# Attention's softmax: dividing the values in place of the weights, and decoding later weights after attention

## The chip, the cores and the metric

The program runs on one core of a Trainium2 chip. A core has TensorE (PE in the rows, with PEld for its weight loads), VectorE (DVE), ScalarE (ACT), GpSimd (POOL) and SyncE (SP), which issues the transfers here. TensorE writes its results to PSUM, which the program uses as eight banks of 128 x 512 float32. The metric is the device time of one execution in microseconds (us); the lower, the better.

## The reference, cut to what matters

Three layers follow one another on 1152 rows of 512 numbers (2 batches x 576 positions, 8 heads x 64):

```python
# attention: a coarse one on means over 4 positions, repeated 4 times, plus a local one (|i - j| < 4)
def sm_attn(qq, kk, vv):
    s = scale * qq @ kk.T
    s = s - max(s)
    a = exp(s)
    a = a / (sum(a) + 1e-09)
    return a @ vv
attn_out = repeat(sm_attn(q_d, k_d, v_d), 4) + sm_attn_masked(q, k, v)
# first layer: h = x @ w_in, g = h * tanh(softplus(h)), x = g @ w_out    (512 -> 2048 -> 512)
# second: 8 experts of 512 -> 1024 -> 512, all on every row, weighted by a gate that is normalised 8 times
out = sum(P[:, e:e + 1] * (relu(x @ w1[e]) @ w2[e]) for e in range(8))
```

`w_in` and `w_out` arrive as float64, so the kernel reads them as pairs of 32-bit words and puts float32 numbers together from them.

## The kernel before, in words

**Three stages.** Attention is worked off in units: eight of the coarse kind (`gunit`: a batch, a half of its rows, four heads) and twelve of the local kind (`lunit`: 96 rows, all heads). Two coarse and three local units run by themselves at the start, with `warm` matmuls of the identity between them. The other units are woven into the first layer in three waves of two coarse and three local units each (the second batch's two halves, and the first batch's second half). The first layer runs over 64 chunks (`s` in the last loop of the quoted code; 12 matmuls of `gemm1`, line 506, then the activation `mish`, then 12 matmuls of `gemm2`, line 529, which belong to the chunk `LAG` = 4 before). The waves cover chunks 0 to 17, and `ATT_END` is 18. Afterwards the first layer runs alone, and then the experts (lines 783 and 821).

**A unit has three steps**: `sc` (scores, lines 321 or 363 and 368, then `softmax`), `tr` (transposes of the weights, line 335 or 379, copied from PSUM by ScalarE, line 337 or 380) and `av` (weights times values, line 347 or 386, then line 349 or lines 392 to 394, which write the first layer's input as a sum of two parts, `xhi` and `xlo`). `piped` puts the steps of different units between each other. `softmax` takes the maximum on VectorE (line 300), the exponentials and their sums on ScalarE (302), adds and inverts the sums (304, 305), and multiplies the weights by the reciprocals on VectorE (307, two instructions a unit).

**Decoding.** A half piece of `w_in` or `w_out` is loaded into one of two buffers (`load_w64`), and `w_raw` makes float32 of it by one ScalarE instruction (180) and three on VectorE (181, 183, 184). When it is done it asks for the load of the half piece four on, which waits until its buffer is free. `w_split` makes two parts of a whole piece (190 on ScalarE, 191 on GpSimd). There are 16 pieces, 32 half pieces; `need` says from which chunk a piece is used, and before the change a half piece is decoded from `AHEAD` = 22 chunks ahead. By the loop that gives the half pieces 12 to 19 to the chunks 7 to 14, under attention; they are used from chunk 24 on.

**What sets the order.** The code is written in program order, but a scheduler reorders the instructions within each engine's queue when the program is built, so the order on the chip is the one in the listings below. Each engine then works its queue off in that order. PSUM banks come in two rings of four, `w` and `acc`. Scores, transposes, values and `gemm1` share the ring `w`, and a bank is free for its next user only when its last reader is done: for `gemm1` that is line 490 of `mish`.

Of the kernel before, what the change touches and what calls it, by code (L numbers as in the profile page):

```python
# [7 lines left out]
F32 = mybir.dt.float32  # L8
# [3 lines left out]
AF = mybir.ActivationFunctionType  # L12
ALU = mybir.AluOpType
# [3 lines left out]
TQ = 96  # L17
# [4 lines left out]
NBUF = 3  # L22
RAWB = 4
ERAW = 3
AHEAD = 22
VWB = 3
PBL, PBG = 6, 4
WARM0, WARM1, WARM2 = 16, 8, 2
# [10 lines left out]
def attn_moe_moe_kernel(  # L39
# [13 lines left out]
    PE, ACT, DVE, POOL, SP = nc.tensor, nc.scalar, nc.vector, nc.gpsimd, nc.sync  # L53
    B, H, S, D = q.shape
# [3 lines left out]
    KD = DM // 128  # L58
# [3 lines left out]
    SD = S // 4  # L62
# [7 lines left out]
    W = TQ + 6  # L70
# [14 lines left out]
    def new(pool, shape, dt, tag, bufs=2):  # L85
        return pool.tile(shape, dt, tag=tag, name=tag, bufs=bufs)
# [15 lines left out]
    POOL.affine_select(out=maskb, in_=maskb, pattern=[[-1, W + 6]], base=9, channel_multiplier=1,  # L102
                       compare_op=ALU.is_ge, fill=NEG)
    vwt = [at.tile([W, H, D], F32, name=f"vw{i}", bufs=1) for i in range(VWB)]
    pl = [at.tile([TQ, H // 2, W], F32, name=f"pl{i}", bufs=1) for i in range(PBL)]
    pg = [at.tile([SH, H // 4, SD], F32, name=f"pg{i}", bufs=1) for i in range(PBG)]
    DVE.memset(two, 2.0)
    DVE.memset(ones, 1.0)
# [10 lines left out]
    def at_bank():  # L119
        state["n"] += 1  # L120
        return bank("acc" if state["start"] and state["n"] % 2 else "w")
# [172 lines left out]
    def softmax(s3, p, rows, tag):  # L294

        n, nh, nk = s3[0].shape
        den = new(at, [n, 2, nh], F32, tag + "d", 2)
        for par in range(2):
            nm = new(at, [n, nh], F32, tag + "m", 4)
            DVE.tensor_reduce(out=nm, in_=s3[par], axis=AX.X, op=ALU.max, negate=True)  # L300
            for i in range(nh):
                exps.append(ACT.activation(out=p[par][:, i], in_=s3[par][:, i], func=AF.Exp, bias=nm[:, i:i + 1],  # L302
                                           scale=1.0, accum_out=den[:, par, i:i + 1]))
        DVE.tensor_scalar(out=den, in0=den, scalar1=1e-9, scalar2=rows, op0=ALU.add, op1=ALU.mult)
        DVE.reciprocal(out=den, in_=den)
        for par in range(2):
            DVE.tensor_tensor(
                out=p[par], in0=p[par], in1=den[:, par].unsqueeze(2).to_broadcast([n, nh, nk]), op=ALU.mult)

    def gunit(b, half, q4):  # L310


        u = {}
        hps = (2 * q4, 2 * q4 + 1)

        def sc():
            bks = [at_bank() for _ in range(2)]
            for i, hp in enumerate(hps):
                for par, bk in enumerate(bks):
                    o = slice(64 * par, 64 * par + 64)  # L320
                    PE.matmul(out=bk[:SH, SD * i:SD * i + SD], lhsT=qd[b, half][o, hp, :], rhs=kd[b][o, hp, :],
                              start=True, stop=True)
            for par in range(2):
                u[par] = pg[state["pg"] % PBG]
                state["pg"] += 1
            softmax([bk[:SH, 0:2 * SD].rearrange("p (a b) -> p a b", b=SD) for bk in bks], u, 4.0, "g")

        def tr():
            u["pt"] = new(at, [W, 8 * TQ], F32, "pt", 2)[:SH, 0:8 * SH].rearrange("p (a b) -> p a b", a=8)
            for par in range(2):  # L330
                bk = at_bank()
                for i in range(2):
                    for c in range(2):
                        j = 2 * i + c
                        PE.transpose(out=bk[:SH, SH * j:SH * j + SH], in_=u[par][:, i, SH * c:SH * c + SH],
                                     identity=ident[:SH, :SH])
                ACT.activation(out=u["pt"][:, 4 * par:4 * par + 4, :].rearrange("p a b -> p (a b)"),
                               in_=bk[:SH, 0:4 * SH], func=AF.Copy)

        def av():  # L340
            if (b, half) not in odT:
                odT[b, half] = new(at, [128, HP, SH], F32, "odT", 1)
            bk = at_bank()
            for i, hp in enumerate(hps):
                for c in range(2):
                    for par in range(2):
                        PE.matmul(out=bk[64 * par:64 * par + 64, SH * i:SH * i + SH], lhsT=vd[b, c][:, 2 * hp + par, :],
                                  rhs=u["pt"][:, 4 * par + 2 * i + c, :], start=(c == 0), stop=(c == 1))
            ACT.activation(out=odT[b, half][:, hps[0]:hps[0] + 2, :].rearrange("p a b -> p (a b)"),
                           in_=bk[:, 0:2 * SH], func=AF.Copy)  # L350
        return [sc, tr, av]

    def lunit(t):

        b, t6, lo, hi = window(t)
        half, t3 = divmod(t6, 3)
        m0 = lo - (TQ * t6 - 6)
        u = {}

        def sc():  # L360
            s3 = [at_bank()[:TQ, 0:4 * W].rearrange("p (a b) -> p a b", b=W) for _ in range(2)]
            for par in range(2):
                PE.matmul(out=s3[par], lhsT=identb[:TQ, :TQ],  # L363
                          rhs=maskb[:TQ, m0:m0 + W].unsqueeze(1).to_broadcast([TQ, 4, W]), start=True, stop=False)
            for hp in range(HP):
                for par in range(2):
                    o = slice(64 * par, 64 * par + 64)
                    PE.matmul(out=s3[par][:, hp, :], lhsT=qT[b, half][o, hp, TQ * t3:TQ * t3 + TQ],  # L368
                              rhs=kT[b][o, hp, lo:hi], start=False, stop=(hp == HP - 1))
            for par in range(2):  # L370
                u[par] = pl[(2 * t + par) % PBL]
            softmax(s3, u, 1.0, "l")

        def tr():
            u["pt"] = new(at, [W, 8 * TQ], F32, "pt", 2)
            for par in range(2):
                bk = at_bank()
                for i in range(HP):
                    PE.transpose(out=bk[:W, TQ * i:TQ * i + TQ], in_=u[par][:, i, :], identity=ident[:TQ, :TQ])  # L379
                ACT.activation(out=u["pt"][:, 4 * TQ * par:4 * TQ * par + 4 * TQ], in_=bk[:W, 0:4 * TQ], func=AF.Copy)  # L380

        def av():
            bk = at_bank()
            for hp in range(HP):
                for par in range(2):
                    PE.matmul(out=bk[64 * par:64 * par + 64, TQ * hp:TQ * hp + TQ], lhsT=vw[t][:, 2 * hp + par, :],
                              rhs=u["pt"][:, TQ * (4 * par + hp):TQ * (4 * par + hp) + TQ], start=True, stop=True)
            y = bk[:, 0:KD * TQ].rearrange("p (a s) -> p a s", a=KD)
            y4 = bk[:, 0:KD * TQ].rearrange("p (a s r) -> p a s r", a=KD, r=4)
            g = odT[b, half][:, :, 24 * t3:24 * t3 + 24]  # L390
            hi_, lo_ = (z[:, :, TQ * t:TQ * t + TQ] for z in (xhi, xlo))
            DVE.tensor_tensor(out=y4, in0=y4, in1=g.unsqueeze(3).to_broadcast([128, KD, 24, 4]), op=ALU.add)
            ACT.activation(out=hi_, in_=y, func=AF.Copy)  # L393
            DVE.tensor_tensor(out=lo_, in0=y, in1=f32(hi_), op=ALU.subtract)
        return [sc, tr, av]
# [197 lines left out]
    for s in range(NS + LAG):  # L593
        if s == NS - 4:
            with tc.issue_after(last["mish"].ins):
                gate()
        for a, b, st in waves:
            if s == b:
                while steps:
                    steps.pop(0)()  # L600
            if s == b == waves[-1][1]:
                at_ctx.close()
                tp = ctx.enter_context(tc.tile_pool(name="tp", bufs=1, side="right", reuse_waits="tile"))
                tx["hi"], tx["lo"] = (tp.tile([128, 3 * KH, NB], F32R, name=f"t{z}") for z in ("hi", "lo"))
            if s == a:
                steps += st
                pump.n, pump.done, pump.at, pump.over = len(steps), 0, 24 * a, FRAC * 24 * (b - a)
        n = place["raw"] // 2
        if n < len(ring) and s >= need[ring[n]] - AHEAD and (s < ATT_END or s % 2 == 0 or s >= need[ring[n]] - 4):
            if s:  # L610
                with tc.issue_after(last["mish"].ins):
                    w_raw()
            else:
                w_raw()
                w_raw()
        n = place["split"]
        if n < len(ring) and 2 * n + 2 <= place["raw"] and free_at(n) <= s:
            w_split()
        if s < NS:
            gemm1(s)  # L620
        if s >= LAG:
            gemm2(s - LAG)
# [269 lines left out]
```

## Time and profile before

| | us |
|---|---|
| median of 3 runs | 1111.71 |
| lowest and highest | 1108.79, 1116.67 |
| the profiled execution | 1111.02 |
| its span, first to last instruction | 1109.2 |
| before the first `gemm1` matmul | 47.9 |
| chunks 0 to 17, with the three waves | some 48 to 187 |

The profiled execution took 1.8 us more than its span and stands 0.7 us under the median. PE is busy in 1077.7 us of the span, DVE in 579.6, ACT in 487.8 and POOL in 368.9, so TensorE bounds the whole. The change touches the first 190 us and, by the decoding, the 60 us behind them. A share of busy time says little there: which engine is waited for has to be read from the waits of that stretch.

### The profile page before, as it was taken

The numbers are of one execution on the slowest core, as the hardware profiler recorded it, in microseconds if no ns is written. First come the engines' busy times: TensorE is split into PE (matmuls) and PEld (weight loads), VectorE is DVE, ScalarE is ACT, GpSimd is POOL, SyncE is SP. The second block draws the span as 40 slices with busy tenths as digits, with TensorE's granted clock in tenths as the row PEclk, the third lists the DMA queues.
The fourth block names the chain that finished last, engine by engine and source line by source line (L and its number), as shares of the span: only waits on it lengthen the run. The fifth ranks groups of instructions, "written<-read, shape, count | busy, mean of one in ns | idle before, by whom it ended". The sixth has DMA issues, their size and how long they took to land.

```text
span 1109.2 us, 18583 instructions
## 1 busy us (share of the span) xinstructions
PE 1077.7 (97%) x7184; PEld 983.7 (89%) x7184; DVE 579.6 (52%) x1229; ACT 487.8 (44%) x1375; POOL 368.9 (33%) x406
## 2 busy tenths in 40 slices
PE   8889999999998999999999999999999999999998
PEld 7768789999998888988989898999888999889897
DVE  4877885545347554454454544435454444444442
ACT  3776777534446443424344242442424434243430
POOL 2444523402217335705134150431505224051300
PEclk9888999999999999999999999999999999999999
DMA  8374320222002102112011111201112011120002
GB/s 189 107 154 120 102 81 20 77 80 74 20 1 76 58 1 77 39 38 76 13 66 39 38 40 38 76 19 58 39 38 76 20 58 38 39 71 20 25 1 86
DMA packets 60196, 63.48 MB, mean 57 GB/s; under 512 B 24204, under 2 KB 44620, under 8 KB 60108
## 3 DMA queue, kind: packets, MB, share of 16 engines
q1 hardware_dynamic: 60108, 62.30, 18.8%
q8 instruction: 56, 0.92, 0.3%
q14 instruction: 32, 0.26, 0.1%
HBM read 59.93 MB, written 2.36 MB: 56 GB/s over the span
## 4 chain that ended last, share of the span: by engine, by line
PE 87%; DVE 4%; ACT 3%; POOL 2%; DMA 2%; issue 1%; POOLq 0%; DVEq 0%
PE w L821 36%; PE acc L783 26%; PE w L506 9%; PE acc L529 8%; PE w L783 4%; PE w L368 1%; ACT pl L302 1%; DMA raw<-in_k_dram 1%; PE acc L442 1%; DMA raw<-in_moe_w_out_dram 0%; POOL wc L695 0%; PE w L363 0%; PE w L379 0%; ACT raw L180 0%; POOL me L487 0%
## 5 line engine op out<-in xcount | busy, mean ns | idle before, releaser
L821 PE MATMUL w<-wc,hhi 128*128 128x512 f32 x1152 | 361.9, 393 | 0.0
L821 PEld LDWEIGHTS w<-wc,hhi 128*128 128x128 f32 x1152 | 210.4, 188 | 37.8
L821 PE MATMUL w<-wc,hlo 128*128 128x512 f32 x576 | 225.2, 391 | 0.0
L695 POOL TENSOR_TENSOR wc<-raw,wc 128x512 fp32r<-128x512 f32 x64 | 82.0, 1305 | 356.1 <-ACT wc L694 355.9
L783 PE MATMUL acc<-thi,wb 128*128 128x288 f32 x768 | 169.0, 295 | 0.0
L783 PE MATMUL acc<-xhi,wb 128*128 128x288 f32 x768 | 167.2, 295 | 1.7 <-DVE xlo L557 1.7
L832 DVE SCALAR_TENSOR_TENSOR yacc<-w,P,yacc 128x512 f32<-128x512 f32 x126 | 94.3, 749 | 81.1 <-PE w L821 81.1
L783 PEld LDWEIGHTS acc<-thi,wb 128*128 128x128 f32 x768 | 128.4, 188 | 3.1
L783 PEld LDWEIGHTS acc<-xhi,wb 128*128 128x128 f32 x768 | 128.1, 188 | 3.1 <-DVE xlo L557 1.9
L821 PEld LDWEIGHTS w<-wc,hlo 128*128 128x128 f32 x576 | 108.1, 188 | 23.8
L770 ACT ACTIVATE p<-acc 128x288 f32<-128x288 f32 x128 | 52.3, 410 | 143.2 <-PE acc L783 139.3
L774 ACT ACTIVATE hhi<-acc 128x288 fp32r<-128x288 f32 x128 | 52.3, 410 | 141.5 <-PE acc L783 117.3
L783 PE MATMUL acc<-xlo,wb 128*128 128x288 f32 x384 | 113.5, 295 | 0.0
L783 PE MATMUL acc<-tlo,wb 128*128 128x288 f32 x384 | 113.1, 295 | 0.0
L683 POOL TENSOR_TENSOR wb<-sums,wb 128x256 fp32r<-128x256 f32 x128 | 93.6, 748 | 53.5 <-ACT wb L682 52.1
L683 POOL TENSOR_TENSOR wb<-raw,wb 128x256 fp32r<-128x256 f32 x96 | 72.5, 758 | 97.4 <-PE acc L783 55.5
L775 DVE SCALAR_TENSOR_TENSOR hlo<-acc,hhi 128x288 fp32r<-128x288 f32 x128 | 58.2, 455 | 77.4 <-ACT hhi L774 74.9
L506 PE MATMUL w<-xhi,hi 128*128 128x288 f32 x256 | 79.4, 311 | 5.3 <-ACT xhi L393 2.9
L506 PE MATMUL w<-xlo,hi 128*128 128x288 f32 x256 | 77.7, 304 | 0.1
L529 PE MATMUL acc<-glo,hi 128*128 128x288 f32 x256 | 76.1, 303 | 1.4 <-POOL glo L494 1.4
L506 PE MATMUL w<-xhi,lo 128*128 128x288 f32 x256 | 77.3, 302 | 0.0
L796 DVE TENSOR_TENSOR acc<-acc,u 128x288 f32<-128x288 f32 x64 | 29.6, 464 | 87.7 <-PE acc L783 87.7
(192 smaller groups left out, 1992.9 us busy)
## 6 DMA issues: line engine op xcount, KB each, us to landing
raw<-in_moe_w_dram SPq DMA_DIRECT2D x64, 512.0 KB
raw<-in_moe_w_in_dram SPq DMA_DIRECT2D x16, 512.0 KB
raw<-in_moe_w_out_dram SPq DMA_DIRECT2D x16, 512.0 KB
vw<-in_v_dram SPq DMA_DIRECT2D x12, 192.0 KB
raw<-in_v_dram SPq DMA_DIRECT2D x8, 288.0 KB
raw<-in_q_dram SPq DMA_DIRECT2D x12, 144.0 KB
out_dram<-yacc SPq DMA_DIRECT2D x6, 256.0 KB
raw<-in_k_dram SPq DMA_DIRECT2D x2, 576.0 KB
```

Of the source, the lines that this page charges most:

```text
L302: exps.append(ACT.activation(out=p[par][:, i], in_=s3[par][:, i], func=AF.Exp, bias=nm[:, i:i + 1], scale=1.0, accum_out=den[:, par, i:i + ...
L506: PE.matmul(out=bk, lhsT=a[:, kk, o], rhs=b[:, kk, c0:c0 + n], start=(i == 0), stop=(i == 3 * KD - 1))
L529: PE.matmul(out=bk, lhsT=a[:, h, o], rhs=b, start=(first and i == 0), stop=(end and i == 2))
L683: POOL.tensor_tensor(out=t[:, 1], in0=src[u][w], in1=f32(t[:, 0]), op=ALU.subtract)
L695: POOL.tensor_tensor(out=t[:, 1], in0=r[:, a], in1=f32(t[:, 0]), op=ALU.subtract)
L770: ACT.activation(out=t, in_=bk[u, b], func=AF.Copy)
L774: ACT.activation(out=hi, in_=y, func=AF.Relu)
L775: DVE.scalar_tensor_tensor(out=lo, in0=y, scalar=0.0, in1=f32(hi), op0=ALU.max, op1=ALU.subtract)
L783: PE.matmul(out=bk[u, b], lhsT=wb[2 * h + u, w][:, wz, kk, :], rhs=ops[xz][:, k + kk, o + c:o + c + NP], start=(m < 3 and i == 0), stop=(i ...
L796: DVE.tensor_tensor(out=bk[u, "C"], in0=bk[u, "C"], in1=kept[u, "u2"], op=ALU.add)
L821: PE.matmul(out=bk, lhsT=a[:, f, 128 * j:128 * j + 128], rhs=w[:, b, :], start=(i == 0), stop=(i == 3 * FH - 1))
L832: DVE.scalar_tensor_tensor(out=y, in0=bk, scalar=p, in1=y, op0=ALU.mult, op1=ALU.add)
```

## The change

The weights stay as the exponentials give them. `softmax` returns the reciprocals (96 or 72 partitions, one column for each head), and `spread` lays each column out: a matmul whose stationary operand is the column repeated 64 times and whose moving operand is the identity puts the reciprocals of one head on 64 partitions, one column for each row of attention. `av` of a coarse unit spreads into its own bank and multiplies by it (ScalarE's copy, then one VectorE multiply). A local unit spreads in `tr` into a bank of its own, which ScalarE copies to `u["r"]` (over the unit's first weight tile), and multiplies its values in `av`. The pieces from the seventh on (half pieces 12 to 31) are decoded from chunk 18 on, one half piece in each chunk.

```diff
@@ softmax
-        den = new(at, [n, 2, nh], F32, tag + "d", 2)
+        den = new(at, [n, 2, nh], F32, tag + "d", 4)
...
         DVE.reciprocal(out=den, in_=den)
+        return den
+
+    def spread(bk, c, den, i):
+
+        n = den.shape[0]
         for par in range(2):
-            DVE.tensor_tensor(
-                out=p[par], in0=p[par], in1=den[:, par].unsqueeze(2).to_broadcast([n, nh, nk]), op=ALU.mult)
+            PE.matmul(out=bk[64 * par:64 * par + 64, c:c + n], lhsT=den[:, par, i:i + 1].to_broadcast([n, D]),
+                      rhs=ident[:n, :n], start=True, stop=True)
@@ gunit, av
-            ACT.activation(out=odT[b, half][:, hps[0]:hps[0] + 2, :].rearrange("p a b -> p (a b)"),
-                           in_=bk[:, 0:2 * SH], func=AF.Copy)
+                spread(bk, 2 * SH + SH * i, u["den"], i)
+            z = odT[b, half][:, hps[0]:hps[0] + 2, :].rearrange("p a b -> p (a b)")
+            ACT.activation(out=z, in_=bk[:, 0:2 * SH], func=AF.Copy)
+            DVE.tensor_tensor(out=z, in0=bk[:, 2 * SH:4 * SH], in1=z, op=ALU.mult)
@@ lunit, tr
+            bk = at_bank()
+            for hp in range(HP):
+                spread(bk, TQ * hp, u["den"], hp)
+            u["r"] = pl[2 * t % PBL].rearrange("p a b -> p (a b)")[:, 0:KD * TQ]
+            ACT.activation(out=u["r"], in_=bk[:, 0:KD * TQ], func=AF.Copy)
@@ lunit, av
+            DVE.tensor_tensor(out=bk[:, 0:KD * TQ], in0=bk[:, 0:KD * TQ], in1=u["r"], op=ALU.mult)
             DVE.tensor_tensor(out=y4, in0=y4, in1=g.unsqueeze(3).to_broadcast([128, KD, 24, 4]), op=ALU.add)
@@ the loop over chunks
-        if n < len(ring) and s >= need[ring[n]] - AHEAD and (s < ATT_END or s % 2 == 0 or s >= need[ring[n]] - 4):
+        if n < len(ring) and s >= (ATT_END if n >= 2 * NBUF else 0):
```

The built programs show where the instructions went. In the changed kernel the lines are numbered anew: 299 stands for 300, 303 and 304 for 304 and 305, 180 to 183 for 181 to 184, 500 to 504 for 488 to 492, 311 is `spread`, 353 is 347, 385 is 379, 518 is 506, and 541 is 529.

The first place is VectorE's queue around the first local unit of the first wave (`lm` are maxima, `ld` sums and reciprocals, `pl` weights, `raw` a piece that is decoded, `mm` and `me` belong to `mish`). Before:

```order
L305 RECIPROCAL ld<-ld 96x8
L300 TENSOR_REDUCE lm<-w 96x4
L307 TENSOR_TENSOR pl_94<-pl_94,ld 96x408
L307 TENSOR_TENSOR pl_95<-pl_95,ld 96x408
L300 TENSOR_REDUCE lm<-w 96x4
L181 TENSOR_SCALAR raw<-raw 128x512
L488 SCALAR_TENSOR_TENSOR mm<-me 128x288
L183 SCALAR_TENSOR_TENSOR raw<-raw_827,raw 128x512
L490 TENSOR_TENSOR me<-mm,w 128x288
```

And now:

```order
L304 RECIPROCAL ld<-ld 96x8
L299 TENSOR_REDUCE lm<-w 96x4
L180 TENSOR_SCALAR raw<-raw 128x512
L299 TENSOR_REDUCE lm<-w 96x4
L182 SCALAR_TENSOR_TENSOR raw<-raw_860,raw 128x512
L183 SCALAR_TENSOR_TENSOR raw<-raw_860,raw 128x512
L500 SCALAR_TENSOR_TENSOR mm<-me 128x288
L502 TENSOR_TENSOR me<-mm,w 128x288
```

The two multiplies are gone, and the decoding's last instruction has moved ahead of `mish`.

The second place is VectorE's queue at the coarse units of the second wave (`gm`, `gd` and `pg` are their maxima, sums and weights). Before:

```order
L181 TENSOR_SCALAR raw<-raw 128x512
L490 TENSOR_TENSOR me<-mm,w 128x288
L304 TENSOR_SCALAR gd<-gd 72x4
L183 SCALAR_TENSOR_TENSOR raw<-raw_1166,raw 128x512
L305 RECIPROCAL gd<-gd 72x4
L184 SCALAR_TENSOR_TENSOR raw<-raw_1166,raw 128x512
L307 TENSOR_TENSOR pg_100<-pg_100,gd 72x288
L307 TENSOR_TENSOR pg_101<-pg_101,gd 72x288
```

And now:

```order
L502 TENSOR_TENSOR me<-mm,w 128x288
L303 TENSOR_SCALAR gd<-gd 72x4
L299 TENSOR_REDUCE gm<-w 72x2
L304 RECIPROCAL gd<-gd 72x4
L504 TENSOR_TENSOR me<-me,ml 128x288
```

Both the decoding and the multiplies are gone from there.

The third place is TensorE's queue at the first `gemm2` (`acc<-ghi`, `acc<-glo`), among the scores of the first wave's coarse units (`w<-kd,qd`). Before:

```order
L321 MATMUL w<-kd,qd 72x144 x2
L529 MATMUL acc<-ghi,hi_835 128x288 x4
L321 MATMUL w<-kd,qd 72x144 x4
L529 MATMUL acc<-glo,hi_835 128x288
L529 MATMUL acc<-ghi,lo_836 128x288
```

And now:

```order
L325 MATMUL w<-kd,qd 72x144 x8
L541 MATMUL acc<-ghi,hi_868 128x288 x4
L518 MATMUL w<-xhi,hi_849 128x288
L518 MATMUL w<-xlo,hi_849 128x288
L518 MATMUL w<-xhi,lo_850 128x288
...
L541 MATMUL acc<-glo,hi_868 128x288
```

Ahead of the first `glo` now stands a whole chunk of `gemm1` (12 matmuls on `xhi` and `xlo`, of which the first three are shown), which stood some ten matmuls behind it before.

## Rows read from the trace of the kernel before

**Rows 1.** The page, part 4: shares of the chain that ended last, by engine

```profile
PE 87%; DVE 4%; ACT 3%; POOL 2%; DMA 2%; issue 1%; POOLq 0%; DVEq 0%
```

**Rows 2.** Four stretches: length, busy us of each engine (x instructions), clock, DMA

```profile
48.00:98.00 50.00, 44.25 (x331) 38.79 (x332) 38.32 (x78) 33.48 (x118) 19.52 (x18) 0.79 0.52 118
98.00:147.00 49.00, 42.69 (x397) 37.24 (x396) 42.19 (x88) 36.54 (x131) 25.11 (x27) 1.00 0.47 129
147.00:190.00 43.00, 42.00 (x377) 38.23 (x376) 30.46 (x69) 32.31 (x118) 12.30 (x13) 0.96 0.13 41
190.00:306.00 116.00, 116.00 (x877) 116.00 (x876) 53.58 (x97) 52.24 (x125) 30.80 (x26) 1.00 0.18 60
```

**Rows 3.** Waits of PE, 48 to 190 us: total, times, longest

```profile
PE w L506 <- ACT xhi L393: 2.9, 2, 1.7
PE acc L529 <- ACT ghi L493: 1.9, 1, 1.9
...
PE acc L529 <- POOL glo L494: 1.4, 2, 0.9
```

**Rows 4.** Stretches of 5 us, the same columns as in rows 2

```profile
60.00:65.00 5.00, 5.00 (x20) 4.35 (x20) 4.00 (x9) 3.32 (x13) 2.08 (x2) 0.50 0.87 166
...
80.00:85.00 5.00, 5.00 (x22) 3.79 (x22) 3.36 (x5) 2.43 (x8) 2.42 (x3) 0.50 0.31 108
85.00:90.00 5.00, 5.00 (x37) 4.66 (x37) 3.76 (x9) 2.95 (x16) 1.19 (x2) 0.56 0.18 58
...
100.00:105.00 5.00, 3.88 (x37) 3.60 (x37) 4.47 (x11) 3.68 (x11) 1.73 (x2) 1.00 0.65 181
105.00:110.00 5.00, 3.84 (x35) 3.46 (x34) 3.58 (x6) 3.12 (x9) 4.11 (x5) 1.00 0.74 200
...
115.00:120.00 5.00, 3.57 (x26) 2.65 (x22) 4.19 (x11) 4.61 (x20) 4.83 (x5) 1.00 0.46 132
120.00:125.00 5.00, 4.13 (x33) 3.27 (x34) 4.96 (x11) 2.56 (x6) 4.34 (x5) 1.00 0.34 105
```

**Rows 5.** PE in order of time: start, us, instruction, [idle before <-releaser]

```profile
76.78 0.87 PE L379 MATMUL w<-ident,pl 96*102 96x96 f32 x8 [0.75 <-ACT pl L302]
78.82 0.40 PE L506 MATMUL w<-xhi,hi 128*128 128x288 f32 x1 [1.17 <-DVE me L490]
```

**Rows 6.** DVE in order of time, the same columns

```profile
74.75 1.86 DVE L307 TENSOR_TENSOR pl<-pl,ld 96x408 f32<-96x408 f32 x2
...
78.33 0.44 DVE L490 TENSOR_TENSOR me<-mm,w 128x288 f32<-128x288 f32 x1
...
79.72 1.07 DVE L307 TENSOR_TENSOR pl<-pl,ld 96x408 f32<-96x408 f32 x2
```

**Rows 7.** Groups by line and shape: xcount | busy us, mean ns | idle

```profile
L184 DVE SCALAR_TENSOR_TENSOR raw<-raw,raw 128x512 uint32<-128x512 uint32 x24 | 17.8, 742 | 0.4
...
L183 DVE SCALAR_TENSOR_TENSOR raw<-raw,raw 128x512 uint32<-128x512 uint32 x24 | 17.4, 725 | 0.4
...
L307 DVE TENSOR_TENSOR pl<-pl,ld 96x408 f32<-96x408 f32 x24 | 17.4, 762 | 0.3
...
L181 DVE TENSOR_SCALAR raw<-raw 128x512 uint32<-128x512 uint32 x24 | 14.0, 584 | 7.3 <-ACT raw L180 6.7
...
L380 ACT ACTIVATE pt<-w 102x384 f32<-102x384 f32 x21 | 9.8, 491 | 3.9 <-PE w L379 2.9 <-PE acc L386 1.1
...
L307 DVE TENSOR_TENSOR pg<-pg,gd 72x288 f32<-72x288 f32 x16 | 8.6, 577 | 0.1
...
L392 DVE TENSOR_TENSOR w<-w,odT 128x384 f32<-128x384 f32 x10 | 5.5, 561 | 2.5 <-PE w L386 2.3
```

**Rows 8.** The chain in order of time: start, us, what

```profile
169.31 0.65 PE w L347 x16
...
178.42 0.81 PE w L386 x16
```

**Rows 9.** The same chain, at the start

```profile
42.41 4.26 DMA raw<-in_moe_w_out_dram
```

More of the change, by code (lines that the diff above doesn't have):

```diff
@@ L24 @@
 ERAW = 3
-AHEAD = 22
 VWB = 3
@@ L104, in attn_moe_moe_kernel @@
     vwt = [at.tile([W, H, D], F32, name=f"vw{i}", bufs=1) for i in range(VWB)]
-    pl = [at.tile([TQ, H // 2, W], F32, name=f"pl{i}", bufs=1) for i in range(PBL)]
+    pl = [at.tile([128, H // 2, W], F32, name=f"pl{i}", bufs=1) for i in range(PBL)]
     pg = [at.tile([SH, H // 4, SD], F32, name=f"pg{i}", bufs=1) for i in range(PBG)]
@@ L325, in sc @@
                 state["pg"] += 1
-            softmax([bk[:SH, 0:2 * SD].rearrange("p (a b) -> p a b", b=SD) for bk in bks], u, 4.0, "g")
+            u["den"] = softmax([bk[:SH, 0:2 * SD].rearrange("p (a b) -> p a b", b=SD) for bk in bks], u, 4.0, "g")
         def tr():
@@ L370, in sc @@
             for par in range(2):
-                u[par] = pl[(2 * t + par) % PBL]
-            softmax(s3, u, 1.0, "l")
+                u[par] = pl[(2 * t + par) % PBL][:TQ]
+            u["den"] = softmax(s3, u, 1.0, "l")
         def tr():
```

## The prediction

> **What bounds the kernel now.** I read the shares of the chain first: 87% of it is TensorE, and no other engine has more than 4% [rows 1]. So the time is TensorE's work plus whatever keeps TensorE waiting or slow. The stretches show where that is. From 190 us on PE and its weight loads are busy in 116.00 of 116 us at the full clock, with VectorE busy in 53.58 [rows 2]: work put there beside TensorE has cover, and nothing can be won there. From 48 to 190 us the three waves of attention run beside chunks 0 to 17, and there TensorE loses time in two ways. It is idle for 5.75, 6.31 and 1.00 us (length less busy in the first three stretches), 13.1 us together. And its granted clock is 0.79 in the first stretch and 0.96 in the third, that is 50 x 0.21 + 43 x 0.04 = 12.2 us of lost pulses [rows 2]. The third wave is otherwise full. So 25.3 us can be won at most in the waves, and all that is added to TensorE there has to be set against it.
>
> The engine behind the waits is mostly VectorE: it is busy in 111.0 of these 142 us, in the second wave in 42.19 of 49 [rows 2], and its queue is strict. Around 75 us the reader sees it plainly: the weights' multiplies (two, 1.86 us) stand ahead of `mish`'s line 490, which frees a PSUM bank at 78.77; TensorE waits 0.75 us for its transposes and 1.17 us for that bank [rows 5, 6], and then works at half its clock for ten microseconds (granted 0.50 and 0.56) [rows 4]. Idle times of 1.12 and 1.16 us in the stretches 100 to 110 were not followed by such a fall, the clock there is 1.00 [rows 4].
>
> **TensorE gets more work.** A local unit's eight `spread` matmuls have the shape of its eight `av` matmuls, 64 columns of stationary and 96 of moving float32; those took 0.81 us at the full clock. A coarse unit's four have the shape of half of line 347's, 0.65 / 2 = 0.33 us [rows 8]. (The trace shows each such matmul as two.) In the waves there are nine local and six coarse units: 9 x 0.81 + 6 x 0.33 = **+9.3 us**. No row shows a repeated column as the stationary operand. The bounds are 0, where the matmuls fall into idle time that stays, and 18.6, where all of them meet the half clock; I take 9.3, because the rows priced from are the nearest in shape and two of three stretches run at nearly full clock. The five units before 48 us add 3.1 us among `warm` matmuls, where TensorE is not what is waited for; their cost is in the start's term.
>
> **VectorE gets less.** In the waves it loses 9 x (2 x 0.762 - 0.561) us for the local units, the new multiply being priced by line 392, which has the same 384 columns in PSUM: 8.7 us. For the coarse ones it loses 6 x (2 x 0.577 - 0.3), where 0.3 is my estimate between 0.15 and 0.561 (144 columns where line 392 has 384): 5.1 us. And half pieces 12 to 19 leave with 8 x (0.584 + 0.725 + 0.742) = 16.4 us [rows 7]. That is 30 us of its 111. ScalarE pays nine copies of 0.49 us for the laid-out reciprocals [rows 7] and loses eight decoding instructions, so it stays as it was. VectorE's time is worth nothing by itself; what TensorE waited for is worked out place by place:
>
> - *The start.* The chain runs through decoding: a piece's load (4.26 us) is asked for when VectorE is done with an earlier half piece [rows 9], and ten multiplies leave that queue. Against it stand one multiply, one copy (0.49) and a spread in the last unit's tail. I take -0.8, between -2.5 and +1.
> - *The first `gemm2`, near 57 us.* Before, TensorE waits 1.9 us for `ghi` and up to 0.9 for `glo` [rows 3]; now a chunk of `gemm1` stands ahead of `glo` (the change's third listing), but the `ghi` wait stays. -1.5. The half clock of the stretch behind it (0.50 from 60 to 65) cost 2.5 us [rows 4]; I count half of it as won, -1.2.
> - *Near 75 us.* Without the multiplies the transposes wait for ScalarE alone, and line 490 comes 1.1 us sooner (1.78 less, but the decoding's last instruction, 0.742 at most, now stands ahead of it, see the first listing) [rows 6, 7]. TensorE meanwhile has 1.1 us of spreads to do, so the bank is there when it comes: the idle 0.75 + 1.17 goes [rows 5], I count -1.6. With it goes the half clock from 80 to 90, 5 x 0.50 + 5 x 0.44 = 4.7 us [rows 4], **-4.7**.
> - *100 to 110 us.* 2.28 us idle [rows 4], with decoding between the preparations of keys and queries. -1.5.
> - *115 to 125 us.* 2.30 us idle [rows 4]; decoding and multiplies are both gone from the queue (second listing), GpSimd's part stays. -1.5.
> - *The waves' ends.* The last local unit's values now pass one multiply more, 0.56 us, before the next wave's first `gemm1` can start; TensorE waits there already, 1.7 us at its longest [rows 3]. Three ends, one with cover: +1.0.
>
> At one of these places a stretched instruction shows: the two multiplies took 1.86 us at 74.75 and 1.07 us at 79.72 [rows 6]. The Trainium skill, page SBUF — State Buffer, section Who interferes with whom, has a VectorE instruction with two SBUF inputs contend with a GpSimd instruction that reads SBUF, and one with a single SBUF input not. The new multiplies read one operand from PSUM, so by that rule GpSimd's `glo` also comes sooner, and both waits for it, 1.4 us together, would go in full: the sum would be 1.4 us lower. The trace agrees as far as line 392 goes, whose mean of 561 ns shows no stretching.
>
> **Decoding behind attention.** Twenty half pieces now come one to a chunk from chunk 18 on. VectorE and ScalarE have room (53.58 and 52.24 of 116 us) [rows 2]. The loop that could be late is that of the two buffers: a load waits for the decoding of the half piece two before. Decoding takes 2.05 us on VectorE and some 0.65 on ScalarE (estimated from line 380's 0.491 for 384 columns), the load at most 4.26 us [rows 7, 9]: 7.0 us for two half pieces. Two chunks take 2 x 24 x 116 / 877 = 6.35 us [rows 2]. So each pair falls behind by up to 0.6 us, over nine pairs 5.6 us. `gemm2` follows `gemm1` by four chunks, 12.7 us, and the tightest piece is asked for some three chunks after its turn, so this is hidden; it costs 0, and up to 5.6 us if ScalarE's queue holds `mish` back longer than that. The attention loads on SP are no longer mixed with loads that wait for decoding: no gain counted.
>
> **The sum.** 9.3 - 0.8 - 1.5 - 1.2 - 1.6 - 4.7 - 1.5 - 1.5 + 1.0 = -2.5 us. From the profiled execution, 1111.0, that gives 1108.5; since that execution stands 0.7 under the median, 1108 to 1109. **I forecast 1108 us, no change that can be told**: 1% of this kernel, 11 us, is about what a measurement can tell from none.
>
> **The rivals.**
>
> *The waves become full.* If every idle time and every slow stretch goes, 25.3 us are won for 9.3 paid, with 2 from the start: 1111 - 18 = 1093. Half way between this and my sum lies 1100. For it speaks that VectorE loses more than a quarter of its load and that falls of the clock multiply what a short wait costs; against it, that part of the waits are on ScalarE's and GpSimd's work, which stays [rows 3]. The Trainium skill, page Perfetto Trace Analysis, section Identifying the Most-Contended Engine, judges TensorE's room by its weight loads and not by its matmuls. By that the room in the waves would be 50 - 38.79 + 49 - 37.24 + 43 - 38.23 = 27.7 us, and this rival would end 2.4 us lower. Chance of ending over 1% faster: 0.23.
>
> *A bank is waited for instead.* Each local unit now takes a sixth bank of the ring `w`, and each unit's `av` bank is held until VectorE has multiplied. If each of the fifteen units in the waves meets one more wait for a bank like the one at 78.82, 1.17 us [rows 5], 17.6 us are added: 1108.5 + 17.6 = 1126. It decides from the point at which a bank is held longer than TensorE takes to come round the ring of four. Against it: that wait came from a VectorE queue that is now emptier. A half of it (1117) is still within 1%. Chance of over 1% slower: 0.10.
>
> *The clock falls anyway.* TensorE's order is new, and a wait of some 2 us at another place would bring back the 4.7 us and leave the idle time: 1108.5 + 6 = 1115. And the decoding's loop, if it shows, gives 1114. Both are within my forecast's 1%.
>
> **How the numbers follow.** Within 1%: 0.67, with the likeliest time 1108. Faster by over 1%: 0.23; slower: 0.10. The range goes from 1098, a little past half way to the full waves, to 1119, where the returned clock loss and some bank waits add up.
>
> **What would show each step.** In the changed profile: 16 rows of line 311 in a local unit, some 0.8 us; the first `gemm1` near 47 us; a granted clock of 1.00 from 80 to 90; no wait of line 518 for line 502 above 0.5 us in the first wave; VectorE busy near 81 us in the waves; the waves ending near 185 us; 116 us of full TensorE behind them, with no wait for decoding. I am wrong if idle time in the waves stays above 10 us, if clock falls show at new places, or if TensorE waits behind chunk 18.

## The result, and the profile after

The changed kernel takes **1121.75 us** (median of 11 runs, 1119.0 to 1126.39) against 1112.95 for the kernel before beside it (11 runs, 1108.79 to 1116.79): a ratio of 1.0082, interval 1.0064 to 1.0099. So it is 0.8% slower, within the 1% that I had called no change, but nearly 14 us above my number and 2.75 above my range. Its profiled execution (1121.9, span 1120.1) stands at the median.

The whole is still TensorE's, by a smaller part of the chain than before [rows 1], with 4% for transfers now:

```profile
PE 84%; DVE 5%; DMA 4%; ACT 3%; issue 2%; POOL 1%; SPq 0%; DVEq 0%; ACTq 0%; POOLq 0%
```

The four stretches of the changed kernel, columns as in [rows 2]:

```profile
48.00:98.00 50.00, 46.33 (x438) 41.40 (x438) 32.85 (x77) 36.93 (x128) 18.36 (x18) 0.91 0.52 126
98.00:147.00 49.00, 44.52 (x436) 39.53 (x435) 25.55 (x62) 34.14 (x124) 21.21 (x25) 0.95 0.27 61
147.00:190.00 43.00, 40.79 (x406) 36.10 (x406) 21.24 (x53) 29.63 (x111) 10.65 (x12) 0.98 0.01 2
190.00:306.00 116.00, 111.15 (x833) 110.21 (x833) 66.42 (x111) 53.72 (x127) 33.48 (x26) 1.00 0.29 96
```

VectorE did get free, 42.19 to 25.55 in the second wave. But the stretch behind 190 us, which was full, has lost 4.85 us of TensorE.

To see where the time goes, I take the start of each chunk (its first `gemm1` matmul) from the time lines of both. The difference to before, in us, in the two profiled executions:

| | changed kernel minus before | added in this part | forecast for it |
|---|---|---|---|
| chunk 0 (48.8) | +0.9 | +0.9 | -0.8 |
| chunk 6, behind the first wave | -3.9 | -4.8 | -5.9 |
| chunk 12, behind the second | -2.9 | +1.0 | +0.1 |
| chunk 19, behind the third | +2.7 | +5.6 | +3.1 |
| chunk 44, behind the decoding | +8.1 | +5.4 | 0 |
| experts, after the gate | +10.9 | +2.8 | 0 |

(The forecast's spreads are shared out by units, 3.1 us a wave, and its +1.0 for the waves' ends is left out. A chunk's first matmul marks progress roughly, since `gemm1` and `gemm2` are ordered anew in each program.) TensorE's waits in the changed kernel from 188 to 250 us, and from 45 to 192 us, in total, times, longest:

```profile
PE acc L541 <- ACT wb L547: 2.7, 2, 1.5
PE w L518 <- ACT hi L189: 2.1, 1, 2.1
...
PE acc L541 <- ACT ghi L505: 2.5, 1, 2.5
PE w L518 <- ACT xhi L405: 2.3, 2, 1.3
```

The first two are new: behind chunk 18 TensorE waits for decoded weights (`hi`, line 189) and for the copies that join the layer's output (`wb`, line 547), 4.8 of the 5.4 us. The waits for `glo` [rows 3] are gone. The granted clock from 80 to 85 us is full where it was 0.50 [rows 4], but the fall at the end of the second wave is longer. The changed kernel's rows, then the last stretch of the kernel before, which had 1.00 from 140 to 145:

```profile
80.00:85.00 5.00, 5.00 (x65) 4.69 (x65) 2.39 (x7) 4.41 (x20) 2.03 (x2) 1.00 0.31 108
140.00:145.00 5.00, 2.57 (x14) 2.55 (x15) 3.35 (x9) 2.24 (x7) 0.80 (x1) 0.71 0.37 84
145.00:150.00 5.00, 5.00 (x29) 5.00 (x29) 0.88 (x2) 2.58 (x7) 0.02 (x1) 0.60 0.00 0
...
145.00:150.00 5.00, 3.49 (x21) 3.50 (x22) 4.71 (x10) 2.89 (x7) 0.80 (x1) 0.74 0.38 84
```

VectorE and ScalarE there, in order of time (the last `av` matmul of the wave ends at 139.95):

```profile
139.98 1.02 DVE L403 TENSOR_TENSOR w<-w,pl 128x384 f32<-128x384 f32 x2
140.91 0.56 DVE L404 TENSOR_TENSOR w<-w,odT 128x384 f32<-128x384 f32 x1
141.37 0.45 DVE L504 TENSOR_TENSOR me<-me,ml 128x288 f32<-128x288 f32 x1
141.74 0.56 DVE L404 TENSOR_TENSOR w<-w,odT 128x384 f32<-128x384 f32 x1
...
141.95 0.43 ACT L505 ACTIVATE ghi<-me 128x288 fp32r<-128x288 f32 x1
142.39 0.49 ACT L405 ACTIVATE xhi<-w 128x384 fp32r<-128x384 f32 x1
```

Two units' new multiplies (line 403) stand ahead of the sum (404), and `mish`'s line 504 and so `ghi` behind them. `xhi` is ready 2.9 us after the last matmul.

The same stands at the start, ahead of chunk 0. TensorE's last rows there, before and now, then VectorE's and ScalarE's of the changed kernel:

```profile
47.91 0.61 PE L506 MATMUL w<-xhi,hi 128*128 128x288 f32 x1 [1.18 <-ACT xhi L393]
...
42.84 0.88 PE L397 MATMUL w<-pt,vw 102*64 102x96 f32 x14 [1.24 <-ACT pt L386]
48.80 0.61 PE L518 MATMUL w<-xhi,hi 128*128 128x288 f32 x1 [5.08 <-DMA raw<-in_moe_w_in_dram]
...
45.38 0.56 DVE L403 TENSOR_TENSOR w<-w,pl 128x384 f32<-128x384 f32 x1
45.85 0.56 DVE L404 TENSOR_TENSOR acc<-acc,odT 128x384 f32<-128x384 f32 x1
46.31 1.37 DVE L182 SCALAR_TENSOR_TENSOR raw<-raw,raw 128x512 uint32<-128x512 uint32 x1
47.60 0.55 DVE L404 TENSOR_TENSOR w<-w,odT 128x384 f32<-128x384 f32 x1
...
48.25 0.49 ACT L405 ACTIVATE xhi<-w 128x384 fp32r<-128x384 f32 x1 [1.26 <-DVE w L404]
```

The last `av` ends at 43.72, 3.0 us sooner than before, but `xhi` is ready at 48.74 only, since new multiplies and decoding stand ahead of the sums in VectorE's queue. TensorE waits 5.08 us where it waited 1.18. (The row puts the wait down to a load that happens to land at 48.79. In all runs chunk 0 starts within 0.06 us of `xhi`.)

The chain of waits behind chunk 18 shows one turn of the decoding:

```profile
206.14 3.56 DMA raw<-in_moe_w_in_dram
...
209.73 0.68 ACT raw L179
...
210.43 0.44 DVE raw L180
...
210.90 0.70 DVE raw L182
...
211.62 1.68 DVE raw L183
...
213.36 3.43 DMA raw<-in_moe_w_out_dram
```

A transfer, one ScalarE and three VectorE instructions, and the next transfer: the turns of one of the two buffers start at 198.77, 206.14, 213.36, 220.73 and 227.88, every 7.3 us for two half pieces. Two chunks take 6.35 [rows 2].

### The profile page after: what moved, and what is told of

It is laid out like the page before. It is cut to its first block, busy times and chain, and to the rows that moved or that the text cites. A ratio compares the mean times of both kernels' runs of the same rounds, so it can differ in the third digit from the quotient of the medians.

```text
span 1120.1 us, 19079 instructions
## 1 busy us (share of the span) xinstructions
PE 1083.5 (97%) x7440; PEld 988.6 (88%) x7440; DVE 566.7 (51%) x1209; ACT 492.8 (44%) x1387; POOL 366.4 (33%) x406
## 4 chain that ended last, share of the span: by engine, by line
PE 84%; DVE 5%; DMA 4%; ACT 3%; issue 2%; POOL 1%; SPq 0%; DVEq 0%; ACTq 0%; POOLq 0%
PE w L833 36%; PE acc L795 26%; PE w L518 6%; PE acc L541 6%; PE w L795 4%; DMA raw<-in_moe_w_in_dram 2%; DMA raw<-in_moe_w_out_dram 1%; PE w L374 1%; DVE raw L183 1%; DMA raw<-in_q_dram 1%; ACT pl L301 1%; PE acc L454 1%; DVE raw L182 1%; PE w L311 0%; ACT raw L179 0%
## 5 line engine op out<-in xcount | busy, mean ns | idle before, releaser
L541 PE MATMUL acc<-ghi,hi 128*128 128x288 f32 x256 | 71.6, 303 | 5.2 <-ACT wb L547 2.7
```

Of the source, the lines that this page charges most:

```text
L541: PE.matmul(out=bk, lhsT=a[:, h, o], rhs=b, start=(first and i == 0), stop=(end and i == 2))
```

## The experiments

My theories were two. **A**: the loss is the decoding's loop behind chunk 18. **B**: it is TensorE's own new work in the waves, and the decoding is harmless. The first four runs undo one part or move one price. Ratios are to the kernel before on the same chip.

**One part each.** `e1_values` has the new softmax and the old rule of decoding:

```diff
-        if n < len(ring) and s >= (ATT_END if n >= 2 * NBUF else 0):
+        if n < len(ring) and s >= need[ring[n]] - AHEAD and (s < ATT_END or s % 2 == 0 or s >= need[ring[n]] - 4):
```

> The new softmax alone; decoding follows the old rule (from 22 chunks ahead). Theory A (the loss is the two-buffer loop of the decoding behind chunk 18, where a load waits for the decoding two half pieces before and TensorE in the end waits for the pieces): no wait of TensorE for the pieces' parts behind chunk 18, the 116 us there full as before, and a time 0 to 5 us over before, ratio 1.000 to 1.005. Theory B (the loss is TensorE's 9.3 us of spreads, and the late decoding helps by relieving VectorE): 9 to 15 us over before, ratio 1.008 to 1.014, chunk 18 reached 5 us or more later than in the kernel before.

`e2_decode` is the other half, the kernel before with the new rule:

> The old softmax with the new rule of decoding (half pieces from the thirteenth on from chunk 18 on). Theory A: chunk 18 is reached 1 to 5 us sooner than before, since 16 us of VectorE's work have left the waves, and the loop behind it loses 5 to 6 us again, with the same wait for a piece near chunk 28; the time 0 to 5 us over before, ratio 1.000 to 1.005. Theory B: no loss behind chunk 18 counts, 3 to 8 us under before, ratio 0.993 to 0.997.

Measured: 1121.42 us, ratio 1.006 (1.004 to 1.008), and 1114.67, 1.0009 (0.9994 to 1.0024). A fits the second run, in its time and place by place; the first lies between the two. The starts of the chunks say why the rule costs nothing by itself: in `e2_decode` the start and the waves up to chunk 19 win 4.5 us, and from there to chunk 44 it loses 5.4 us, just what the changed kernel loses there; `e1_values` loses 0.4 there. (These are differences of single executions; that of `e1_values` took 1115.73, 5.7 us under its median.)

**More of the spreads.** `e4_twice` issues each spread twice:

```diff
+            for _ in range(2):
                 PE.matmul(out=bk[64 * par:64 * par + 64, c:c + n], lhsT=den[:, par, i:i + 1].to_broadcast([n, D]),
```

> The changed kernel with each spread matmul issued twice with the same result; prices the spreads. If TensorE pays for them in full in the waves, chunk 18 is reached 8 to 11 us later than in the changed kernel and the time is 8 to 12 us over it, ratio to before 1.015 to 1.019. If they fall into TensorE's idle time, under 4 us over it, ratio under 1.012. Theory B needs the first, theory A takes either.

1128.41 us, 1.0139 (1.0114 to 1.0163), between the two expectations: the second set costs 0.57%, some 6 us, where its matmuls make 9.3 in the waves and 3.1 at the start. TensorE pays about half of them.

**Decoding earlier.** `e6_from12` is the changed kernel with the later pieces from chunk 12 on:

```diff
-        if n < len(ring) and s >= (ATT_END if n >= 2 * NBUF else 0):
+        if n < len(ring) and s >= (12 if n >= 2 * NBUF else 0):
```

> The changed kernel with one number changed: the later pieces are decoded from chunk 12 on, not 18, so that the first six half pieces are done beside the third wave. Theory A: the waits for a piece's parts and for copies held up by the decoding's ScalarE instruction behind chunk 18 vanish, 4 to 7 us under the changed kernel, ratio to before 1.001 to 1.005. Theory B: the ratio stays within 1.007 to 1.011, or grows as VectorE's work comes back into the third wave.

1118.16 us, 1.0039 (1.0021 to 1.0057), with 0.3 us lost from chunk 19 to 44. So by the ratios the decoding behind chunk 18 is some 4.8 us of the loss (0.43%), and 4.3 are left.

**What makes the loop long.** In the turn above line 183 takes 1.68 us, where it takes 0.69 at other times. `e5_dvesub` has VectorE do line 190's subtraction, which GpSimd did beside it:

```diff
-            POOL.tensor_tensor(out=lo[:, c], in0=raw[:, c], in1=f32(hi[:, c]), op=ALU.subtract)
+            (DVE if place["split"] > 6 else POOL).tensor_tensor(out=lo[:, c], in0=raw[:, c], in1=f32(hi[:, c]), op=ALU.subtract)
```

> The changed kernel, but for the pieces from the seventh on the second part of the split (line 190) is subtracted on VectorE instead of GpSimd. Theory S (line 183's 1.67 us beside GpSimd's subtraction, where it takes 0.69 alone, makes the pair of half pieces 7.4 us long instead of some 6.6): TensorE loses 0 to 3 us between the chunks 18 and 36 instead of 5.4, total 1114 to 1119, ratio 1.000 to 1.005. Rival (the transfer and the two buffers alone make the loop late): 5 us lost there as before, total 1120 to 1124, ratio 1.006 to 1.010.

1117.05 us, 1.0038 (1.0018 to 1.0058), as theory S expected. Line 183 is at 0.69, and the stretch from 190 to 306 us is full again although VectorE has more to do:

```profile
L183 DVE SCALAR_TENSOR_TENSOR raw<-raw,raw 128x512 uint32<-128x512 uint32 x12 | 8.2, 686 | 0.2
...
190.00:306.00 116.00, 115.66 (x874) 115.46 (x873) 70.40 (x136) 56.27 (x131) 6.08 (x7) 1.00 0.31 96
```

Nothing is lost there from chunk 19 to 44. But that does not show the stretching to be the whole cause. Line 190 now stands in VectorE's queue (0.68 us), and a turn takes 6.8 us (for every second half piece line 183 starts at 199.70, 206.10, 213.59, 220.61 and 227.00): shorter than 7.3, and still longer than two chunks, 6.35. ScalarE still waits for loads. What is gone is what stood behind them, for the program is ordered anew. ScalarE's rows of `e5_dvesub`, then of the changed kernel:

```profile
217.87 0.67 ACT L179 ACTIVATE raw<-raw 128x512 f32<-128x512 f32 x1 [2.15 <-DMA raw<-in_moe_w_out_dram]
...
236.24 1.00 ACT L547 ACTIVATE wb<-acc 128x288 f32<-128x288 f32 x3
...
242.04 0.66 ACT L179 ACTIVATE raw<-raw 128x512 f32<-128x512 f32 x1 [1.60 <-DMA raw<-in_moe_w_in_dram]
242.60 0.70 ACT L547 ACTIVATE wb<-acc 128x288 f32<-128x288 f32 x2
```

Three join copies now stand ahead of a decoding instruction, not behind it. And TensorE, which waited for the second half of chunk 28's weights, has twelve matmuls of `gemm2` between the two halves: that half is ready 2.35 us after the chunk's start (3.04 in the changed kernel), and nothing waits. How much of the gain is the shorter turn and how much the order was not separated.

**Old softmax, decoding from chunk 12.** `e7_old12` is the kernel before with `e6_from12`'s rule:

> The kernel before with its old softmax; only the decoding rule is new: half pieces 12 to 31 from chunk 12 on, one to a chunk. Theory A (the two-buffer decoding loop behind chunk 18 costs 5.4 us and a clock fall in the gate's stage some 3 us more; both vanish when it starts six chunks earlier): the 4.5 us that the waves won in the run with the old softmax and the new rule stay, so 1105 to 1109, ratio 0.993 to 0.997. Rival (decoding in the third wave costs there what the loop costs behind it): 1113 to 1116, ratio 0.999 to 1.002.

1120.48 us, 1.0067 (1.0046 to 1.0088): both expectations failed. The loss stands at one place, 8.8 us up to chunk 36. ScalarE's decoding waits for a load and holds the join copies behind it, and TensorE waits 4.17 us and then works at half its clock (granted 0.50 from 240 to 245 us). ScalarE's rows, then TensorE's:

```profile
237.97 0.66 ACT L180 ACTIVATE rawx<-raw 128x512 f32<-128x512 f32 x1 [1.61 <-DMA raw<-in_moe_w_out_dram]
239.15 0.99 ACT L535 ACTIVATE wb<-acc 128x288 f32<-128x288 f32 x3
...
239.60 0.61 PE L529 MATMUL acc<-ghi,hi 128*128 128x288 f32 x1 [4.17 <-ACT wb L535]
240.01 0.44 PE L529 MATMUL acc<-glo,hi 128*128 128x288 f32 x1
```

So starting earlier cures the late weights and not the held queue. In `e6_from12` the decoding waits for loads at the same place, but the copies came in time; why the loop stands differently there was not tried.

**Which units.** From here on the question was which part of the softmax costs. Theory **P**: the spread matmuls. Theory **Q**: the copy and the multiply at the ends of the units. `e8_coarse12` (from chunk 12) leaves the local units as they were before:

```diff
@@ softmax
         DVE.reciprocal(out=den, in_=den)
+        if tag == "l":
+            for par in range(2):
+                DVE.tensor_tensor(
+                    out=p[par], in0=p[par], in1=den[:, par].unsqueeze(2).to_broadcast([n, nh, nk]), op=ALU.mult)
@@ lunit
-            bk = at_bank()
-            for hp in range(HP):
-                spread(bk, TQ * hp, u["den"], hp)
-            u["r"] = pl[2 * t % PBL].rearrange("p a b -> p (a b)")[:, 0:KD * TQ]
-            ACT.activation(out=u["r"], in_=bk[:, 0:KD * TQ], func=AF.Copy)
...
-            DVE.tensor_tensor(out=bk[:, 0:KD * TQ], in0=bk[:, 0:KD * TQ], in1=u["r"], op=ALU.mult)
```

> Decoding from chunk 12 on; only the coarse units divide their values, the local units multiply their weights as before. Theory P (TensorE pays the spread matmuls of the waves; 9 x 0.81 = 7.3 of the 9.3 us are the local units'): 5 to 8 us below the run with all units new and decoding from chunk 12 (1118.2), so 1108 to 1113, ratio 0.996 to 1.000. Theory Q (the loss is at the units' ends, where the copy of the reciprocals and one more multiply stand before the layer's input): the local units are the ones at the waves' ends, so nearly the same, 1108 to 1113; what tells P from Q is the run without spreads. Rival (the coarse units' change is the costly one): 1115 to 1119.

1105.1 us, **0.9932** (0.9911 to 0.9953), below the expected range: against `e6_from12` the local units' change costs 1.07%, some 12 us. `e11_coarse` is the kernel before, its old rule of decoding with it, and only the coarse units changed:

> The kernel before with its old decoding rule; only the coarse units divide their values. Theory V (the coarse units' change pays by itself: 2 us of spreads for 5.1 us of VectorE's time, and the transposes wait for ScalarE alone): 3 to 6 us below before, 1107 to 1111, ratio 0.995 to 0.998. Rival (it pays only together with the new decoding rule, which empties VectorE's queue in the second wave): 1112 to 1115, ratio 0.999 to 1.002.

1108.6 us, 0.9957 (0.9938 to 0.9977): the coarse units' change pays by itself. `e9_none12` keeps copies and multiplies, and puts one bf16 matmul of the identity in the place of each pair of float32 spreads, so it leaves out the division:

```diff
-        for par in range(2):
-            PE.matmul(out=bk[64 * par:64 * par + 64, c:c + n], lhsT=den[:, par, i:i + 1].to_broadcast([n, D]),
-                      rhs=ident[:n, :n], start=True, stop=True)
+        PE.matmul(out=bk[:, c:c + n], lhsT=identb[:n, :], rhs=identb[:n, :n], start=True, stop=True)
```

> All units new, decoding from chunk 12, but the float32 spread matmuls are replaced by one bf16 matmul of the identity for each pair of heads: the copies and multiplies stay, the division of the values by the right sums is left out. Theory P (TensorE pays the spreads nearly in full): three quarters or more of the 9.3 us go, so 5 to 9 us below the run with spreads (1118.2): 1109 to 1113, ratio 0.995 to 0.999. Theory Q (copy and multiply at the units' ends cost, not the matmuls): 1116 to 1119, ratio 1.002 to 1.004.

1115.6 us, 1.0027 (1.0011 to 1.0043), Q's value: 0.12% below `e6_from12`, which the intervals don't tell from nothing. The row of its waits from 45 to 192 us, and its first stretch, with that of `e6_from12` behind it:

```profile
PE w L516 <- ACT xhi L403: 8.4, 4, 3.4
...
48.00:98.00 50.00, 46.56 (x346) 41.08 (x347) 31.36 (x69) 34.05 (x119) 19.23 (x18) 0.75 0.51 117
48.00:98.00 50.00, 45.32 (x418) 40.33 (x419) 31.84 (x74) 35.72 (x125) 18.39 (x18) 0.90 0.57 131
```

The 8.4 us stand at the four places where `gemm1` needs a wave's last `xhi`. TensorE's waits there in four runs and in the kernel before, in us (at the second end also for `ghi`):

| | chunk 0 | first end | second | third | together |
|---|---|---|---|---|---|
| before | 1.18 | 0 | 1.73 | 0 | 2.9 |
| `e8_coarse12`, local units as before | 1.19 | 0 | 1.66 | 0 | 2.9 |
| `e12_unread` (below), spreads alone | 2.27 | 0 | 1.76 | 0 | 4.0 |
| `e9_none12`, copy and multiply alone | 3.4 | 0.4 | 2.7 | 1.9 | 8.4 |
| `e6_from12`, both | 4.5 | 1.0 | 2.5 | 1.7 | 9.7 |

So the waits come with the copy and the multiply, and without the matmuls nearly all of them stay. The matmuls' own time did not come back as a gain: in this execution the clock of the first stretch is 0.75, where it is 0.90 in `e6_from12`, which is 7.5 us; but this execution stands 3.7 us above its median, so what took the gain in the others is not shown. `e12_unread` is the reverse, `e8_coarse12` with the local units' spreads issued and never read:

```diff
+            bk = at_bank()
+            for hp in range(HP):
+                spread(bk, TQ * hp, u["den"], hp)
```

> As the run with only the coarse units new and decoding from chunk 12 (1105.1), but the local units also issue their eight spread matmuls into a bank of their own, which nobody reads: they multiply their weights as before. Theory P (the matmuls are what the local units' change costs): most of the 13 us to the run with all units new come back, 1113 to 1119, ratio 1.000 to 1.005. Theory Q (the copy of the reciprocals and the multiply at the units' ends cost): at most half of the matmuls' 7.3 us show, 1105 to 1109, ratio 0.993 to 0.997.

1113.22 us, 0.9991 (0.9968 to 1.0014): 0.59%, some 6.6 us, above `e8_coarse12`, at the edge of P's range and above Q's. So both are true, and they do not add: matmuls alone 0.59%, copy and multiply alone (`e9_none12`, against `e8_coarse12`) 0.95%, both 1.07%. (`e9_none12` has the coarse units without their float32 spreads too.) Why they do not add is not shown.

**A version that beats both.** `e10_slow` is `e8_coarse12`, but the four pieces that are needed from chunk 48 on are decoded in every second chunk:

```diff
-        if n < len(ring) and s >= (12 if n >= 2 * NBUF else 0):
+        if n < len(ring) and s >= (12 if n >= 2 * NBUF else 0) and (n < 12 or s % 2 == 0):
```

> The kernel with only the coarse units new and decoding from chunk 12, but the last four pieces (needed from chunk 48 on) are decoded only in every second chunk. Theory A (ScalarE's decoding instruction waits for a load and holds the copies that join the layer's output, at chunk 36): the wait for the join copies and the waits of ScalarE for loads behind chunk 24 go, 0 to 2 us below the run without this edit (1105.1): 1103 to 1106, ratio 0.991 to 0.995. Rival (the loads, now in every second chunk, fall into the gate's and the experts' loads): 1106 to 1110.

**1103.87 us, 0.9915 (0.9886 to 0.9943)**: faster than before and after. That it is better than `e8_coarse12` the intervals don't show. Its stretch behind the waves is full, and no wait for join copies is left (`e8_coarse12` had one of 1.0 us):

```profile
190.00:306.00 116.00, 116.00 (x878) 116.00 (x877) 53.71 (x98) 49.09 (x118) 27.92 (x22) 1.00 0.20 60
```

## Why the prediction was wrong, step by step

**What bounds the kernel, and VectorE's relief**: right; what the relief was worth, too large. From 48 us to the end of the waves, before and now:

```profile
48.00:185.80 137.80, 124.82 (x1070) 110.38 (x1071) 109.47 (x230) 98.97 (x358) 56.12 (x55) 0.91 0.39 102
...
48.00:188.30 140.30, 129.94 (x1263) 115.33 (x1263) 78.31 (x189) 99.01 (x360) 49.41 (x54) 0.94 0.28 67
```

VectorE is busy in 78.3 us (forecast 81). Idle time of TensorE fell from 13.0 to 10.4 us and the clock's loss from 137.8 x 0.09 = 12.4 to 140.3 x 0.06 = 8.4: 6.6 us won. The terms of the waves other than the spreads came to 11.0. Of the three signs that I had named for being wrong, two came: idle time above 10 us in the waves (10.4), and TensorE waiting behind chunk 18; the clock fell at an old place, but for longer.

**TensorE gets more work, +9.3**: right in size. Groups of the changed kernel in the waves:

```profile
L311 PE MATMUL w<-ident,ld 96*64 96x96 f32 x144 | 8.5, 263 | 0.2 <-DVE me L502 0.2
...
L403 DVE TENSOR_TENSOR w<-w,pl 128x384 f32<-128x384 f32 x9 | 5.0, 562 | 5.9 <-PE w L397 5.9
L391 ACT ACTIVATE pl<-w 128x384 f32<-128x384 f32 x9 | 4.4, 490 | 1.1 <-PE w L311 1.1
L311 PE MATMUL w<-ident,gd 72*64 72x72 f32 x48 | 3.5, 226 | 0.0
...
L356 DVE TENSOR_TENSOR odT<-w,odT 128x144 f32<-128x144 f32 x6 | 1.6, 269 | 0.2 <-ACT odT L355 0.2
```

The matmuls overlap. From the first of them to the next operation a local unit's take 0.71 or 0.81 us (1.34 once, where the clock was low), a coarse unit's 0.35 to 0.45 in two parts: 7.4 + 2.2 = 9.6 in the waves. Multiplies and copies have the forecast's prices, 0.562 for 0.561, 0.269 for 0.3, 0.490 for 0.491.

**The first `gemm2`, near 75 us and its clock**: right. The first wave won 4.8 us net, forecast 5.9. The clock is full from 80 us on (from 75 to 80 it is 0.77, where the kernel before had 0.91), and of the idle 1.92 us there 0.9 is left. (Line 490 comes 1.78 - 0.742 = 1.04 us sooner by those rows, not 1.1; nothing hangs on it.) I had said by the Trainium skill (SBUF — State Buffer, Who interferes with whom) that both waits for `glo` would go in full; they are gone in the changed kernel. That this is the rule's doing is not shown: a chunk of `gemm1` now stands ahead of the first `glo`.

**The waves' ends, +1.0**: too small. TensorE waits 1.01 us at the first end, 2.48 at the second and 1.28 at the third, 4.8 where before it was 1.73; and the second end's wait is followed by a clock loss of 5 x 0.29 + 5 x 0.40 = 3.5 us (1.7 in the third stretch before, [rows 2]): together +4.8. I had added one multiply of 0.56 to the path. It is two, since the last two units end together, and `mish`'s line 504 stands behind them in VectorE's queue. That the tail makes these waits, and not the matmuls, is shown by `e9_none12`: 5.0 us at the three ends without the spreads, 5.2 with them (`e6_from12`).

**The start, -0.8**: +0.9 came. It is one more unit's end, and its tail was sized too small: I had set one multiply, one copy and a spread against the gain, and the wait for `xhi` grew by 3.9 us (5.08 for 1.18). Where the local units are as before, it is 1.19 (`e8_coarse12`, `e11_coarse`) and chunk 0 begins at 46.2 and 46.8. The spreads cost there too: chunk 0 begins 2.8 us later in `e12_unread` than in `e8_coarse12`, and 5.5 us later in `e4_twice` than in the changed kernel. These are single executions: `e5_dvesub` is written differently from the changed kernel only for the pieces behind the waves, and its chunk 0 begins 2.3 us later.

**Decoding behind attention, 0**: this step failed, with +5.4 us. The size of the loop was right (7.0 us forecast, 7.3 measured), but by luck: the load took some 3.5 us and not 4.26, and line 183 took 1.68 and not 0.725. With the right load the sum would have been 6.2, and no lag at all. What was wrong is the cover that I took: "`gemm2` follows `gemm1` by four chunks, 12.7 us, and the tightest piece is asked for some three chunks after its turn". The first late piece is one of `w_in`, which `gemm1` itself uses (2.1 us at chunk 28), so `gemm2`'s four chunks do not cover it. The half pieces that came before were already late, a piece is used only after its split, and the wait went up ScalarE's queue. There the decoding's first instruction waits up to 2.1 us for a load, and the copies of line 547, which I had not named, stand behind it. And there was a stretching that I had read elsewhere and not applied here. Line 183 has two SBUF inputs and runs beside GpSimd's line 190, which reads SBUF: 1.68 us, and 0.686 without it (`e5_dvesub`). By these rows a turn without it would take some 6.3 us, an estimate, just under two chunks; no run has the changed loop without it and otherwise alike. The rule of the Trainium skill (SBUF — State Buffer, Who interferes with whom) says that such a pair contends; the trace agrees. I had given its other half without its condition: with one SBUF input an instruction does not contend "outside the 2-port perf modes". The rivals' sentence "the decoding's loop, if it shows, gives 1114" thus had the mechanism, and only the sum left it out.

**The gate's stage, not in the sum**: +2.8 us. TensorE waits there for the gate, 2.1 and 2.5 us, in the kernel before as well, and its granted clock fell after them in some executions and not in others: 0.96 from 345 to 440 us here and in `e2_decode`, 1.00 in the kernel before, `e1_values` and `e6_from12`. I can't tie it to the change, and single executions can't show how often it comes.

So the 13.4 us between forecast and profiled execution are 5.4 of decoding, 3.5 in the waves (their ends), 1.7 at the start and 2.8 at the gate. That decoding behind chunk 18 and the local units' change cost is shown by experiments (`e1_values`, `e2_decode` and `e6_from12`; `e8_coarse12`). How the local units' part divides between spreads and tail, and how the gate's divides between the change and one execution's luck, stays open.

## What to carry to other kernels

One and the same edit paid in the coarse units (0.43% faster by themselves) and cost 1.07% in the local ones, which stand at the ends of the waves: price each kind of unit by itself, and by what comes after it. When work is moved behind a busy stage, write down its period against that of its consumer, with each instruction's price beside the neighbours that it will have there, and list what is queued behind the instruction that waits. And an operation taken off the bounding engine need not give its time back: without the float32 spreads the kernel was no faster that can be told (0.12%), and the waits for the units' tails stayed (8.4 of 9.7 us).

## What the runs showed that I had not expected

The stretching is mutual, and it also takes an instruction with one SBUF input, which the prediction had put as free of it. VectorE and GpSimd in the decoding of the changed kernel, in order of time:

```profile
210.43 0.43 DVE L180 TENSOR_SCALAR raw<-raw 128x512 uint32<-128x512 uint32 x1 [0.23 <-ACT raw L179]
...
211.62 1.67 DVE L183 SCALAR_TENSOR_TENSOR raw<-raw,raw 128x512 uint32<-128x512 uint32 x1
...
214.54 1.07 DVE L180 TENSOR_SCALAR raw<-raw 128x512 uint32<-128x512 uint32 x1 [0.89 <-ACT raw L179]
...
211.00 1.74 POOL L190 TENSOR_TENSOR lo<-raw,hi 128x512 fp32r<-128x512 f32 x1 [2.90 <-ACT hi L189]
214.03 1.30 POOL L190 TENSOR_TENSOR lo<-raw,hi 128x512 fp32r<-128x512 f32 x1 [1.29 <-ACT hi L189]
```

Line 180 takes 0.43 us alone and 1.07 when it starts during GpSimd's subtraction. GpSimd's own time is 1.30 when it came first and 1.74 when VectorE's line 182 was under way. And with less work for TensorE its granted clock from 48 to 98 us was lower, 0.75 in `e9_none12` for 0.90 in `e6_from12`. That the one comes of the other is not shown: single executions scatter nearly as much (0.84 in `e8_coarse12` and 0.94 in `e10_slow`, whose programs are written alike up to chunk 23).
